# Holding weight loads back, one DMA server in the planner, and r and v loads issued from ScalarE

## The chip, the cores and the metric

The kernel runs on one core of one Trainium2 chip. The metric is device time in microseconds (us), the median of several executions. The span of a profile is about 2 us shorter than the time of its own execution (4 us below the median in the first profile of the kernel before, whose execution was a faster one); positions in a profile are counted from the start of the span.

Engine names: PE is TensorE's matmul, PEld its weight load, DVE is VectorE, ACT is ScalarE, POOL is GpSimd, SP is SyncE. A trailing q (SPq, ACTq) means the engine's sequencer, where DMA issues run.

## The reference

Two parts follow one another. A recurrence over 768 steps for 4 batches and 8 heads of 40 channels, and then a mixer over its output:

```python
for t in range(S):                                   # state: (B, H, D, D)
    y[:, :, t] = einsum('bhd,bhde->bhe', r_t, state)
    Sa = einsum('bhde,bhe->bhd', state, a_t)
    state = state * w_t[..., None] - einsum('bhd,bhe->bhde', Sa, b_t)
    state = state + einsum('bhd,bhe->bhde', v_t, k_t)
# x = y as (B, S, 320)
theta = x @ w_theta
u = x + w_tok_r @ (x * cos(theta)) + w_tok_i @ (x * sin(theta))   # over tokens
out = u + maximum(u @ w_ch, 0)
```

The kernel works on 24 chunks (4 batches of 6 chunks of 128 tokens). A chunk needs six loads of 160 KB (r, k, v, w, a, b): 144 loads. After the 6 chunks of a batch come the mixer rows of that batch.

## The kernel before

Every operation is entered in a planner, which simulates the engines and writes one static order for each engine. The kernel then issues the operations in that order. The parts that matter here:

```python
class Plan:
    def order(self, wait=47.7, tswitch=11847.0):
        ...
            elif o.work:                               # a DMA
                q = 0 if o.eng == "SP" else 1          # two servers: SP's and POOL's
                iss = 430 if o.eng == "SP" else 890
                free[o.eng] = t + iss
                s = max(dma[q], t + iss + 900)
                ...
                o.end = dma[q] + 1000
        ...
        out.sort(key=lambda o: (o.start, o.idx))
        return out
...
    raw_w = sb("raw_w", [128, H, D], FP32, 4)          # raw_a, raw_kb, raw_rv: four of each too
...
    def loads(i):                                      # w, k, b, a, r, v of chunk i
        for key, dst, src in load(i):
            add("SP", "load", i, lambda dst=dst, src=src: nc.sync.dma_start(out=dst, in_=src),
                430, [], [key], work=910)
...
    def prep(i):
        add("ACT", "ln", i, ...)        # lw <- raw_w, the first step of a chunk
        ...                             # cs (PE), exp (ACT), kb, ah (POOL, DVE for i < 2), rv casts
        tr("tkb", "ekb", ...); tr("ta", "ea", ...); tr("trv", "erv", ...)
                                        # transposes on PE, evictions kbT, aT, rvT on ACT
...
    def wtok_block(tb):                 # token weights: 2 rows of 192 KB in each of 6 blocks
        add("POOL", "wdma", i, ... nc.gpsimd.dma_start(...), 890, [], [...], work=1100)
...
    order = plan.order()
    for o in order:
        ...
        o.fn()
```

The `x0` matmuls (`ps_s<-rv,psi`) are the first step of a chunk's recurrence; I use their start as the clock of the pipeline. Chunk 8's `x0` comes at about the time when the first mixer rows (`ps_s<-zr,wtok_r`) start.

Of the kernel before, what the change touches and what calls it, by code (L numbers as in the profile page):

```python
# [12 lines left out]
ALU = mybir.AluOpType  # L13
# [4 lines left out]
LAT = {("PE", "ACT"): 36, ("PE", "DVE"): 38, ("ACT", "PE"): 52, ("DVE", "PE"): 52,  # L18
       ("POOL", "PE"): 53, ("ACT", "DVE"): 33, ("ACT", "POOL"): 77}
OVERLAP = {"ACT": 94, "DVE": 83, "POOL": 50}  # L20
FREE0 = {"PE": 800, "ACT": 2100, "DVE": 4400, "POOL": 3600, "SP": 740}
BANKS = 8
DOUBLE = 4


class Op:
    __slots__ = ("eng", "kind", "i", "fn", "cost", "tail", "reads", "writes", "prio",
                 "mode", "table", "new", "spare", "pre", "nsucc", "start", "end", "idx",
                 "npre", "succ", "work", "banks", "soft", "loose")


class Plan:
# [7 lines left out]
    def add(self, eng, kind, i, fn, cost, reads=(), writes=(), prio=0.0, mode=128,  # L40
            tail=0, table=None, new=None, spare=0, work=0, after=(), loose=False):
        o = Op()
        o.eng, o.kind, o.i, o.fn, o.cost, o.prio = eng, kind, i, fn, cost, prio
        o.mode, o.tail, o.table, o.new, o.spare, o.work = mode, tail, table, new, spare, work
        o.reads, o.writes, o.loose = reads, writes, loose
        o.idx = len(self.ops)
        pre = set(after)
        for r in reads:
            if r in self.writer:
                pre.add(self.writer[r])  # L50
        for w in writes:
            if w in self.writer:
                pre.add(self.writer[w])
            pre.update(self.readers.get(w, ()))
        for r in reads:
            self.readers.setdefault(r, []).append(o)
        for w in writes:
            self.writer[w] = o
            self.readers[w] = []
        pre.discard(o)  # L60
        o.pre = list(pre)
        self.ops.append(o)
        return o

    def order(self, wait=47.7, tswitch=11847.0):
        ops = self.ops
        for o in ops:
            o.succ = []
            o.npre = len(o.pre)
            o.start = o.end = None  # L70
            o.banks = None
        users = {}
        for o in ops:
            for k in set(o.reads) | set(o.writes):
                if k[0] == "ps":
                    users.setdefault(k, set()).add(o)
# [7 lines left out]
        for o in ops:  # L84
            for p in o.pre:
                p.succ.append(o)
            for p in o.soft:
                p.succ.append(o)
        left = {k: len(v) for k, v in users.items()}
# [8 lines left out]
        dma = [0.0, 0.0]  # L98
# [9 lines left out]
        def make_ready(o):  # L108
            t = 0.0
            for p in o.pre:  # L110
                t = max(t, lat(p, o))
            est0[o] = t
            ready[o.eng].append(o)
# [17 lines left out]
        while len(out) < n:  # L131
            pick = None
            for e, lst in ready.items():
                if not lst:
                    continue
                te = free[e]
                cand = []
                lo = None
                for o in lst:
                    t = max(te, est0[o])  # L140
                    b = None
                    if o.new is not None:
                        f = find(o)
                        if f is None:
                            continue
                        t = max(t, f[0])
                        b = f[1]
                    if e == "PE" and o.mode != mode:
                        t += 91
                    cand.append((t, o, b))  # L150
                    if lo is None or t < lo:
                        lo = t
# [3 lines left out]
                for t, o, b in cand:  # L156
                    s = o.prio + wait * (t - lo)
                    if e == "ACT" and o.table is not None and o.table != table:
                        s += tswitch
                    if best is None or (s, o.idx) < best[0]:  # L160
                        best = ((s, o.idx), t, o, b)
# [19 lines left out]
            elif o.work:  # L181
                q = 0 if o.eng == "SP" else 1
                iss = 430 if o.eng == "SP" else 890
                free[o.eng] = t + iss
                s = max(dma[q], t + iss + 900)
                if q == 1 and dma[0] > s:
                    dma[0] += o.work
                    dma[1] = s + 2 * o.work
                else:
                    dma[q] = s + o.work  # L190
                o.end = dma[q] + 1000
            else:
                o.end = t + o.cost
                free[o.eng] = o.end - OVERLAP[o.eng]
# [23 lines left out]
def tail(n):  # L218
# [3 lines left out]
OFF = dict(load=-32.72, ln=-14.21, cs=-14.27, exp=-12.91, kb=-24.2, ah=-17.45, rv=-8.81,  # L222
           tkb=-12.03, ekb=-12.49, ta=-6.68, ea=-13.73, spsi=-4.74, mpsi=3.81, sphi=-3.67,
           mphi=-0.3, trv=-7.1, erv=-4.13, slv=-1.2, mlv=12.94, x0=-1.29, nx=-1.28,
           nu=-1.19, enu=-4.96, gt=3.22, egt=5.53, gd=-0.91, egd=-4.34, nut=0.71,
           enut=-1.87, slu=0.59, mlu=4.85, y=4.31, ex=0.1, xt=7.27, ext=6.43, th=11.06,
           eth=17.93, sin=5.35, z=1.67, row=13.39, uadd=1.12, ut=13.16, eut=16.3, ch=19.9,
           oo=11.33, st=19.28, wdma=-32.85, wt=-13.25, ewt=-5.52)
PERIOD = 7.54
ROWLAG = 7.44  # L230
ROWSTEP = 7.6
# [3 lines left out]
def kernel(  # L235
# [130 lines left out]
    def prio(kind, i):  # L366
        return 1000.0 * (PERIOD * i + OFF[kind])

    def add(eng, kind, i, fn, cost, reads=(), writes=(), pr=None, **kw):
        return plan.add(eng, kind, i, fn, cost, tuple(reads), tuple(writes),  # L370
                        prio(kind, i) if pr is None else pr, **kw)
# [16 lines left out]
    def evac(eng, kind, i, psk, dst, n, reads=(), writes=()):  # L388
        if eng == "ACT":
            add(eng, kind, i, lambda: copy_words(dst, ps(psk)[:, 0:n // 2]),  # L390
                190 + n / 2.4, [psk], writes)
# [4 lines left out]
    def loads(i):  # L396
        for key, dst, src in load(i):
            add("SP", "load", i, lambda dst=dst, src=src: nc.sync.dma_start(out=dst, in_=src),  # L398
                430, [], [key], work=910)

    def prep(i):
# [6 lines left out]
            out=lw[:, :, 0:D], in_=raw_w[s4], func=AF.Ln), 465,  # L408
# [3 lines left out]
        def cs():  # L412
# [17 lines left out]
            out=ex, in_=ps(pk)[:, :, 0:328], func=AF.Exp), 740, [pk], [kex], table="lnexp")  # L430
# [3 lines left out]
        for j, nm in enumerate("kb"):  # L434
# [3 lines left out]
                490 if fast else 830, [("raw_" + nm, s4), kex], [("kb", j, i % NKB)])  # L438
# [3 lines left out]
            490 if fast else 830, [("raw_a", s4), kex], [("ah", i % 3)])  # L442
# [18 lines left out]
    def scores(i, kind, kindm, lhs, rhs, keys, dst, dkey, mask):  # L461
        p = ("ps", kind, i)

        def go():
# [7 lines left out]
        add("PE", kind, i, go, 8 * 28, keys, [p], new=(p, 2), mode=64, tail=tail(128))  # L472
# [3 lines left out]
            in1=mask.to_broadcast([128, 2 * G, 128]), op=ALU.mult), 1222, [p], [dkey])  # L476
# [11 lines left out]
    def recurrence(i):  # L488
# [9 lines left out]
        def x0():  # L498
# [16 lines left out]
            455, [pk], [("nx", s2)])  # L515

        def nu_mm():
# [8 lines left out]
            mul=-1.0), 480, [pk], [("nu", s2)])  # L526
        if not last:
            gk = ("ps", "gt", i)

            def gt_mm():  # L530
# [29 lines left out]
                340, [dk], [("gd", i % 2)])  # L560
# [5 lines left out]
    def x_transposed(kind, kinde, i, src, skey, dst, dkey, eng="ACT", pr=None):  # L566
        p = ("ps", kind, i)

        def go():
# [4 lines left out]
        add("PE", kind, i, go, 3 * mm(128), [skey], [p], pr=pr, new=(p, 1), tail=tail(128))  # L574
        d = dst.rearrange("p a b -> p (a b)")
        add(eng, kinde, i, lambda: copy_words(d, ps(p)[:, 0:192]), 345, [p], [dkey],
            pr=None if pr is None else pr + 500)

    def readout(i):
# [9 lines left out]
        def y():  # L589
# [21 lines left out]
            op=ALU.mult), 480, [pk, ("ex", i % NEX)], [("x", i % NX)])  # L611
# [7 lines left out]
    def theta(i):  # L619
# [4 lines left out]
        if i == N - 1:  # L624
            return
        add("ACT", "eth", i, lambda: nc.scalar.copy(out=th_t[0][:, j], in_=ps(pk)[:, 0:DM]),
            455, [pk], [("th", j)])

    def sines(bi, js):
        cs = cs_t[js[0] // 3]  # L630
        i = bi * NCH + js[-1]
        for c in range(2):
# [6 lines left out]
            else:  # L639
# [3 lines left out]
                    190 + 267 * len(js), [("th", j) for j in js],  # L643
# [16 lines left out]
    def mix_row(bi, j):  # L660
        q = bi * NCH + j
        base = 1000.0 * (PERIOD * (bi * NCH + NCH - 1) + ROWLAG + ROWSTEP * j + OFF["row"])
# [5 lines left out]
        for n, s in enumerate(order):  # L668
# [7 lines left out]
            if n == 0:  # L676
                need += [e for e in zk if e[3] <= (NT - 2 if bi < B - 1 else NT - 2)]
            add("PE", "row", q, chunk, 2 * mm(320), need, [pk], pr=base,
# [3 lines left out]
            out=u[:, 0:DM], in0=ps(pk)[:, 0:DM], in1=x[:, 0:DM], op=ALU.add), 480,  # L682
            [pk, ("x", q % NX)], [("u", q % 4)], pr=base + 1000 * (OFF["uadd"] - OFF["row"]))
        x_transposed("ut", "eut", q, u, ("u", q % 4), uT_t[q % 2], ("uT", q % 2),
                     pr=base + 1000 * (OFF["ut"] - OFF["row"]))
        ck = ("ps", "ch", q)
        add("PE", "ch", q, lambda: mix3(ps(ck)[:, 0:DM], uT_t[q % 2], wch), 3 * mm(320),
            [("uT", q % 2), ("wch", 0), ("wch", 1)], [ck], pr=base + 1000 * (OFF["ch"] - OFF["row"]),
# [4 lines left out]
            op1=ALU.add), 480, [ck, ("u", q % 4)], [("oo", q % 3)],  # L693
            pr=base + 1000 * (OFF["oo"] - OFF["row"]))
        add("SP", "st", q, lambda: nc.sync.dma_start(out=out_r[bi, j], in_=oo), 430,
            [("oo", q % 3)], [], pr=base + 1000 * (OFF["st"] - OFF["row"]), work=470)

    def mixer_weights():
        for dst, key, src in ((wth, "wth", moe_w_theta), (wch, "wch", moe_w_ch)):
# [5 lines left out]
            add("POOL", "wdma", 0, go, 890, [], [(key, 0)], work=500, pr=-500.0 if key == "wth" else 1e4)  # L705
            add("POOL", "wdma", 0, go2, 890, [], [(key, 1)], work=130, pr=-500.0 if key == "wth" else 1e4)

    def wtok_block(tb):
        i = 7 + tb
        for nm, ap in (("r", moe_w_tok_r), ("i", moe_w_tok_i)):  # L710
            row = wrow[nm][tb % 2]
            add("POOL", "wdma", i, lambda row=row, ap=ap: nc.gpsimd.dma_start(
                out=row, in_=ap[tb * 128:(tb + 1) * 128, :]), 890, [],
                [("wrow", nm, tb % 2)], work=1100)
# [86 lines left out]
```

## Time and profile before

| | before |
|---|---|
| time, median of 2 | 223.26 us |
| span | 219.2 us |
| first x0 | 16.7 us |
| x0 of chunk 8 | 76.4 us (7.5 us a chunk) |
| first mixer row | 73.6 us |

The page of the kernel before: busy time, then rows in which each digit is the busy share in tenths of one fortieth of the span.

```profile
PE 198.0 (90%) x3368; PEld 155.4 (71%) x3368; DVE 167.2 (76%) x250; ACT 147.1 (67%) x319; POOL 119.2 (54%) x184
...
PE   1519999889987999999999999999999999999992
...
PEclk9999999999999999999999999999999999999999
DMA  6999999999999899999999999999980000100121
```

The same in four stretches of time (start and end, length, then busy time of each engine with the number of instructions, clock, DMA share, GB/s), kernel before:

```profile
0.00:16.00 16.00, 4.49 (x44) 3.39 (x45) 7.72 (x47) 4.75 (x9) 6.78 (x20) 1.00 1.01 167
16.00:75.00 59.00, 53.28 (x993) 42.84 (x993) 47.58 (x57) 44.02 (x95) 36.82 (x56) 1.00 1.04 173
75.00:214.00 139.00, 138.90 (x2327) 108.74 (x2325) 110.48 (x144) 98.01 (x216) 75.59 (x109) 1.00 0.67 127
```

From 75 us on TensorE is the limit: 138.9 of 139 us. What can be won lies before, above all in the first 16 us. The chain of waits (start, length, what) says what holds the start up in the kernel before:

```profile
6.03 9.44 DMA raw_w<-in_w_dram
15.47 0.02 issue
15.50 0.48 ACT lw L407
```

w of chunk 1 takes 9.4 us to land, while GpSimd has asked for 968 KB of mixer weights besides w_theta. ScalarE meanwhile is early with chunk 0 (timeline: start, length, engine, line, operation; in brackets the idle time before it and what ended it), kernel before:

```profile
3.69 0.47 ACT L407 ACTIVATE lw<-raw_w 128x320 bf16<-128x320 f32 x1 [1.67 <-DMA raw_w<-in_w_dram]
...
9.17 0.37 ACT L383 COPY aT<-ps_s 128x256 f32<-128x256 f32 x1 [1.13 <-PE ps_s L380]
```

The PEclk row reads 9 from the start, and the stretches read 1.00, but the clock record of this run begins only at 21.9 us. Two groups of eight transposes, same shape, in the timeline of the kernel before:

```profile
6.38 1.04 PE L380 MATMUL ps_s<-ident,kb 128*128 128x128 bf16 x8 [1.34 <-DVE kb L436]
...
64.36 0.61 PE L380 MATMUL ps_s<-ident,rv 128*128 128x128 bf16 x8 [0.68 <-ACT nuT L383]
```

Their starts are 107 ns apart before 21.9 us and 56 ns after it: TensorE ran at half clock until then, and the PEclk row does not show it.

### The profile page before, as it was taken

The page shows a single profiled execution, that of the slowest core. Times are in us where ns is not written, and L with a number is a line of the kernel's source. Part 1 is how long each engine was busy: PE and PEld are TensorE (multiplying, and loading weights), DVE is VectorE, ACT ScalarE, POOL GpSimd, SP SyncE. Part 2 cuts the span into 40 slices and gives each one's busy share as a digit, 9 for nine tenths or more (in the row PEclk, how much of TensorE's full clock was granted, in tenths as well). Part 3 has the DMA queues.
Part 4 walks back from the last instruction along what each step waited for, and adds up shares of the span by engine and source line. Part 5 has one row for each costly group of instructions (what it writes and reads, how often), then busy time and mean ns, then how long its engine had stood idle before and what let it go on. Part 6 is the DMA issues. An engine that isn't in the chain of part 4 may idle for free.

```text
span 219.2 us, 8154 instructions
## 1 busy us (share of the span) xinstructions
PE 198.0 (90%) x3368; PEld 155.4 (71%) x3368; DVE 167.2 (76%) x250; ACT 147.1 (67%) x319; POOL 119.2 (54%) x184
## 2 busy tenths in 40 slices
PE   1519999889987999999999999999999999999992
PEld 1418778667776788878778778877877788776671
DVE  7336899885898759898598878869888889975532
ACT  3316755886769984996689766987698759563110
POOL 5600536798737791794938644986187507514000
PEclk9999999999999999999999999999999999999999
DMA  6999999999999899999999999999980000100121
GB/s 113 199 185 191 154 168 174 176 178 152 174 187 170 152 172 185 153 155 189 191 187 155 178 189 183 167 184 190 178 182 33 3 33 30 34 33 30 64 88 60
DMA packets 155684, 30.81 MB, mean 141 GB/s; under 512 B 150400, under 2 KB 155648, under 8 KB 155648
## 3 DMA queue, kind: packets, MB, share of 16 engines
q1 hardware_dynamic: 153216, 27.54, 68.9%
q0 software_dynamic: 2432, 2.77, 8.0%
q8 instruction: 26, 0.43, 0.8%
q14 instruction: 10, 0.08, 0.1%
HBM read 29.13 MB, written 3.93 MB: 151 GB/s over the span
## 4 chain that ended last, share of the span: by engine, by line
PE 74%; DMA 7%; DVE 6%; POOL 3%; ACT 3%; issue 3%; SPq 2%; DVEq 0%; ACTq 0%; POOLq 0%
PE ps_s L671 18%; PE ps_s L380 15%; PE ps_d L468 11%; PE ps_s L616 9%; DMA raw_w<-in_w_dram 7%; PE ps_s L572 4%; PE ps_s L538 2%; PE ps_s L520 2%; SPq L398 2%; PE ps_s L602 2%; PE ps_s L508 2%; DVE lamu L473 2%; PE ps_s L600 2%; DVE psi L473 2%; PE ps_s L502 1%
## 5 line engine op out<-in xcount | busy, mean ns | idle before, releaser
L436 POOL TENSOR_TENSOR kb<-raw_kb,ex 128x320 bf16<-128x320 f32 x44 | 37.1, 863 | 49.7 <-ACT ex L429 49.1
L671 PE MATMUL ps_s<-zr,wtok_r 128*128 128x320 bf16 x144 | 40.8, 300 | 0.0
L671 PE MATMUL ps_s<-zi,wtok_i 128*128 128x320 bf16 x144 | 40.7, 299 | 0.0
L473 DVE TENSOR_TENSOR lamu<-ps_d,mask_p 128x1024 bf16<-128x1024 f32 x24 | 29.3, 1221 | 5.3 <-PE ps_d L468 4.6
L473 DVE TENSOR_TENSOR psi<-ps_d,mask_p 128x1024 bf16<-128x1024 f32 x24 | 29.2, 1216 | 5.3 <-PE ps_d L468 5.3
L473 DVE TENSOR_TENSOR lamv<-ps_d,mask_p 128x1024 bf16<-128x1024 f32 x24 | 29.2, 1218 | 5.0 <-PE ps_d L468 2.7
L473 DVE TENSOR_TENSOR phi<-ps_d,mask_n 128x1024 bf16<-128x1024 f32 x24 | 29.3, 1219 | 1.9 <-PE ps_d L468 1.6
L445 POOL CAST rv<-raw_rv 128x320 bf16<-128x320 f32 x44 | 19.1, 452 | 16.0 <-DMA raw_rv<-in_r_dram 8.8
L652 POOL TENSOR_TENSOR zr<-cs,x 128x320 bf16<-128x320 f32 x23 | 17.9, 792 | 10.3 <-ACT cs L640 10.2
L383 ACT COPY rvT<-ps_s 128x512 f32<-128x512 f32 x24 | 14.2, 590 | 9.2 <-PE ps_s L380 9.0
L383 ACT COPY uT<-ps_s 128x192 f32<-128x192 f32 x24 | 7.7, 320 | 17.4 <-PE ps_s L572 13.9
L429 ACT ACTIVATE ex<-ps_d 128x656 f32<-128x656 f32 x24 | 17.2, 718 | 2.9 <-PE ps_d L424 2.0
L383 ACT COPY kbT<-ps_s 128x512 f32<-128x512 f32 x24 | 14.0, 584 | 7.5 <-PE ps_s L380 7.1
L440 POOL TENSOR_TENSOR ah<-raw_a,ex 128x320 bf16<-128x320 f32 x22 | 19.0, 866 | 0.0
L468 PE MATMUL ps_d<-aT,kbT 64*128 64x128 bf16 x384 | 18.3, 223 | 0.7 <-ACT aT L383 0.5
L380 PE MATMUL ps_s<-ident,kb 128*128 128x128 bf16 x192 | 15.9, 227 | 2.5 <-DVE kb L436 1.3
L652 POOL TENSOR_TENSOR zi<-cs,x 128x320 bf16<-128x320 f32 x23 | 17.9, 793 | 0.0
L681 DVE TENSOR_TENSOR u<-ps_s,x 128x320 bf16<-128x320 f32 x24 | 11.8, 490 | 8.0 <-PE ps_s L671 7.5
L671 PEld LDWEIGHTS <-wtok_r 128*128 128x128 bf16 x144 | 14.0, 98 | 4.5
L671 PEld LDWEIGHTS <-wtok_i 128*128 128x128 bf16 x144 | 14.1, 98 | 3.8
L407 ACT ACTIVATE lw<-raw_w 128x320 bf16<-128x320 f32 x24 | 11.2, 478 | 7.6 <-DMA raw_w<-in_w_dram 7.4
L691 DVE SCALAR_TENSOR_TENSOR oo<-ps_s,u 128x320 f32<-128x320 f32 x24 | 11.7, 488 | 5.8 <-PE ps_s L616 5.1
(109 smaller groups left out, 552.6 us busy)
## 6 DMA issues: line engine op xcount, KB each, us to landing
raw_w<-in_w_dram SPq DMA_DIRECT2D x24, 160.0 KB, 4.0
raw_kb<-in_k_dram SPq DMA_DIRECT2D x24, 160.0 KB, 4.1
raw_kb<-in_b_dram SPq DMA_DIRECT2D x24, 160.0 KB, 3.9
raw_a<-in_a_dram SPq DMA_DIRECT2D x24, 160.0 KB, 4.0
raw_rv<-in_r_dram SPq DMA_DIRECT2D x24, 160.0 KB, 3.9
raw_rv<-in_v_dram SPq DMA_DIRECT2D x24, 160.0 KB, 3.7
out_dram<-oo SPq DMA_DIRECT2D x24, 160.0 KB, 1.9
wrow_r<-in_moe_w_tok_r_dram POOLq DMA_DIRECT2D x6, 192.0 KB, 4.7
```

The lines of the kernel that those rows point to most:

```text
L380: nc.tensor.transpose(out=dst[:, c:c + 128], in_=pair(src, g), identity=ident)
L383: nc.scalar.copy(out=out.bitcast(FP32), in_=in_)
L429: add("ACT", "exp", i, lambda: nc.scalar.activation(out=ex, in_=ps(pk)[:, :, 0:328], func=AF.Exp), 740, [pk], [kex], table="lnexp")
L436: lambda j=j: (nc.vector if fast else nc.gpsimd).tensor_tensor(out=kb[:, j, :, 0:D], in0=raw_kb[s4][:, j], in1=invW, op=ALU.mult),
L440: lambda: (nc.vector if fast else nc.gpsimd).tensor_tensor(out=ah[:, :, 0:D], in0=raw_a[s4], in1=Wi, op=ALU.mult),
L445: lambda j=j: (nc.scalar.copy if fast else nc.gpsimd.tensor_copy)(out=rv[:, j, :, 0:D], in_=raw_rv[s4][:, j]),
L468: nc.tensor.matmul(t[:, q, g, :], lhsT=lhs[rows(q), g * 128:(g + 1) * 128], rhs=rhs[rows(q), g * 128:(g + 1) * 128], start=True, stop=True)
L473: add("DVE", kindm, i, lambda: nc.vector.tensor_tensor(out=dst.rearrange("p a b c -> p (a b) c"), in0=ps(p).rearrange("p a (g c) -> p (a g ...
L616: nc.tensor.matmul(dst, lhsT=lhs[:, kt, :], rhs=rhs[:, kt, :], start=kt == 0, stop=kt == 2)
L652: nc.vector if fast else nc.gpsimd).tensor_tensor(
L671: nc.tensor.matmul(ps(pk)[:, 0:DM], lhsT=wtok[nm][:, s, j * 128:(j + 1) * 128], rhs=zs[c][:, s], start=n == 0 and c == 0, stop=n == NT - 1 ...
L681: add("DVE", "uadd", q, lambda: nc.vector.tensor_tensor(out=u[:, 0:DM], in0=ps(pk)[:, 0:DM], in1=x[:, 0:DM], op=ALU.add), 480, [pk, ("x", ...
```

## The change

The intent: (1) hold the mixer weights back by release times, so that they don't stand in the way of the first chunks; (2) let the planner model all loads as served by one DMA server; (3) take the issue of r and v loads (46 of 144, all but chunk 0's) off SyncE and give it to ScalarE's DMA queue. All priorities were set anew with it.

```diff
+SP_DEPTH = 3600.0
...
-            t = 0.0
+            t = 0.0 if o.release is None else 1000.0 * TIMES["rel"][o.release]
...
                 te = free[e]
+                if e == "SP":
+                    te = max(te, dma - SP_DEPTH)
...
-                q = 0 if o.eng == "SP" else 1
-                iss = 430 if o.eng == "SP" else 890
-                free[o.eng] = t + iss
-                s = max(dma[q], t + iss + 900)
-                ...
+                free[o.eng] = t + o.cost
+                if o.eng in ("SP", "ACT"):
+                    dma = max(dma, t + 1350.0) + o.work
+                    o.end = dma + 600.0
+                else:
+                    s = max(t + 1800.0, dma - SP_DEPTH)
+                    dma = max(dma, s) + o.work
+                    o.end = min(dma, s + 2.0 * o.work) + 1000.0
...
     def loads(i):
         for key, dst, src in load(i):
-            add("SP", "load", i, lambda dst=dst, src=src: nc.sync.dma_start(out=dst, in_=src),
-                430, [], [key], work=910)
+            act = key[0] in ("raw_r", "raw_v") and i > 0
+            eng = nc.scalar if act else nc.sync
+            add("ACT" if act else "SP", "load", i,
+                lambda dst=dst, src=src, eng=eng: eng.dma_start(out=dst, in_=src),
+                100 if act else 650, [], [key], work=1030)
...
+            add("POOL", "wdma", 2 + tb, ..., 580, [], [...], at="rel", work=1240, release=2 + tb)
```

Note what the planner now believes: a load on SyncE waits until the server is less than 3.6 us behind; a load on ScalarE costs 0.1 us and never waits.

## The prediction

> **What bounds it now.** The page: span 219.2 us (time 223.26), TensorE busy 198.0 us (90%). Busy time by stretch: in 75–214 us TensorE is busy 138.9 of 139, clock 1.00, so that stretch is TensorE-bound. Before it, TensorE is busy 4.5 of the first 16 us and 53.3 of the next 59; the end leaves 4 us idle. So about 21 us are winnable, 11.5 of them in start-up. The chain of waits names the start-up: raw_w of chunk 1 is issued at 6.03 us and lands 9.4 us later, because GpSimd has queued the mixer weights and four 192 KB token-weight rows between 2.8 and 9 us. The queue of DMA issues shows SyncE's own issues at 2.8 and 3.8 us each there, 0.73 us median overall. Loads move at about 0.91 us per 160 KB (175–180 GB/s).
>
> **What changes.** Work on all compute engines is the same (3368 matmuls; switches between 64- and 128-row matmuls 136 to 132[...]). Moved:
> 1. Token weights and wch go out later. By itself: the 7.6 us of DMA they took early leave chunk 1's path; worth up to 5 us.
> 2. 46 of 144 loads (r, v from chunk 1 on) go to ScalarE's queue: at 0.5–0.7 us an issue, about 25–30 us more on ScalarE, busy 147 of 219 (80% in 75–175 us).
> 3. The whole static order changes.
>
> [...] DMA busy share of 0.97–1.19 before 150 us agrees: no bandwidth is gained. [...]
>
> **The step that decides.** ScalarE is in order, and the eight completion semaphores (the trace shows eight) are now shared by both issuers: each load waits for the one eight places earlier. In the new ScalarE order six r/v loads stand before the first ln, two of them waiting for earlier landings (ln of chunk 0 near 7.5 us instead of 3.7). Fifteen r/v loads, up to chunk 11, stand before the eviction of aT of chunk 0. The last of them needs r of chunk 7 landed and cast; that is the 29th load: about 2.75 + 29×0.91 + 1.3 (theta weights) = 30 us (estimate). In before aT of chunk 0 was evicted at 9.2 us and its x0 matmuls ran at 16.7; I expect these x0 matmuls at about 33 us. Loads of chunks 0–3 are then all there, so chunks go at 6.5–7.5 us each (7.5 in before). Mixer rows start after the x0 of chunk 8: at about 90–94 us against 73.6. From there before took 145.6 us; after has 94 matmuls fewer left: about 141.5. Sum 232–236 us span, plus 4 us outside the span.
>
> **Prediction: 237 us** (6% slower), range 227 to 250. Chances: faster by over 2% 0.09, within 2% 0.11, slower by over 2% 0.80.
>
> **Would show it right:** TensorE nearly idle until about 28–33 us; first x0 matmuls after 28 us; ScalarE idle or inside load issues then; loads of r for chunks 9–11 issued before aT of chunk 0; first mixer matmuls at 88–96 us; TensorE over 97% busy from 100 us on; ScalarE issues 0.5–1 us each. **Wrong:** first x0 matmuls before 22 us.
>
> **What would make it wrong.** ScalarE issues costing about 0.1 us and loads landing faster than 0.91 us; chunks 0–5 catching up at 5 us each since their data wait in SBUF (then 222–226); a faster dense stretch. On the other side: ScalarE, with its issues, becoming the limit in the dense stretch (245–250).

The sum runs: first x0 at about 33 us, first mixer row at about 90 to 94, 141.5 us from there to the end, so 232 to 236 us of span, and 4 us outside it (223.26 less 219.2). Two figures in it come from the trace of the kernel before: the first load landed at 3.66 us, that is 2.75 + 0.91. The 1.3 us for w_theta (200 KB; 1.1 us at 0.91 us per 160 KB) and the 0.5 to 0.7 us an issue were my estimates; SyncE's 144 load issues in that trace took 0.37 us at least and 0.73 us in the median.

## The result

| | before | after |
|---|---|---|
| time, median of 2 | 223.26 us | 258.23 us |
| span | 219.2 us | 257.4 us |
| first x0 | 16.7 us | 33.4 us |
| x0 of chunk 8 | 76.4 us | 110.9 us |
| from there to the end of the span | 142.8 us | 146.5 us |
| first mixer row | 73.6 us | 112.5 us |

The ratio is 1.160 (95% interval 1.150 to 1.171). Ratios here are the mean time of one kernel's fast runs over that of the other's of the same rounds, so not quite the ratio of the medians that I quote.

The 38.2 us of span (3 us more than the 35.0 us between the medians, see above) split into 16.7 us in the start, 17.8 us between x0 of chunk 0 and x0 of chunk 8 (77.5 against 59.7 us) and 3.7 us after it. The page of the kernel after:

```profile
PE 207.4 (81%) x3368; PEld 163.4 (63%) x3368; DVE 166.5 (65%) x250; ACT 147.2 (57%) x319; POOL 120.1 (47%) x184
...
PE   0341168969889639779999998999999989999993
...
PEclk9999999986999975999999999999999999999999
DMA  9999996798619999339479998999470000001112
```

The same work (3368 matmuls) takes 9.4 us more busy time, and the PEclk row has holes at the ninth and tenth and at the fifteenth and sixteenth digit. In stretches, kernel after:

```profile
0.00:33.00 33.00, 7.13 (x68) 5.25 (x68) 7.65 (x47) 6.42 (x12) 7.98 (x23) 1.00 1.36 175
33.00:112.50 79.50, 61.86 (x1044) 49.74 (x1045) 52.56 (x61) 46.14 (x99) 37.95 (x58) 0.89 0.84 134
112.50:252.00 139.50, 136.99 (x2254) 107.69 (x2250) 104.92 (x141) 94.00 (x207) 74.19 (x105) 1.00 0.53 100
```

The start is as predicted: DMA is never idle from 1.8 us on (175 GB/s, so two issuers move no more than one did at 167 to 173), but TensorE has nothing to do. ScalarE's timeline in the kernel after says why (ACTq rows are DMA issues):

```profile
25.69 0.58 ACT L399 COPY rvT<-ps_s 128x512 f32<-128x512 f32 x1 [3.01 <-DMA raw_w<-in_w_dram]
27.07 3.92 ACTq L417 DMA_DIRECT2D raw_rv<-in_r_dram  x3
31.02 0.37 ACT L399 COPY aT<-ps_s 128x256 f32<-128x256 f32 x1 [4.75 <-issue]
```

The eviction of aT of chunk 0, at 9.17 us before, comes at 31.02 us, behind fifteen r and v loads. ScalarE also waits for landings of loads that have nothing to do with its next operation (rvT "released" by raw_w). That is the wait of a load issue: in the trace the 168 loads and stores of both queues use eight completion semaphores in turn, 21 times each, and an issue waits for the load that had its semaphore before, eight places earlier in that turn. Of ScalarE's 14 issues that waited over 0.5 us, 12 went 0.02 to 0.10 us after that landing. The last of the fifteen, r of chunk 11, waited for its buffer: r of chunk 7 landed at 28.82 us, its cast on GpSimd ended at 29.41, and the issue began at 29.45.

The middle is not as predicted. ScalarE's two longest single waits from 33 to 112.5 us (engine, line, what it waited for, total, times, longest), kernel after; three groups of shorter waits, for TensorE's products, have more in total:

```profile
ACT nu L543 <- DMA raw_kb<-in_k_dram: 3.8, 1, 3.8
ACT rvT L399 <- DMA raw_w<-in_w_dram: 3.3, 1, 3.3
```

and the chain of waits of the kernel after in that place:

```profile
91.57 4.58 DMA raw_kb<-in_k_dram
96.14 0.03 ACTq L417
96.17 0.18 ACT nuT L399
96.36 0.05 issue
96.40 0.61 PE ps_d L487 x6
```

A k load lands, ScalarE's issue (ACTq) goes, the eviction behind it goes, TensorE goes. From x0 of chunk 0 (33.4 us) to 112.5 us ScalarE had 16 load issues; they were waited for 7.8 us, all of it between 84 and 102 us, and took 6.2 us (summed from the trace). And TensorE was at half clock until 45.7 us, at 56.0 to 62.8 and at 93.5 to 103.8 us: 29.4 us of the 77.5 between x0 of chunk 0 and of chunk 8. The transposes show it where the PEclk row does not (kernel after, compare with 0.61 us above):

```profile
39.64 1.26 PE L396 MATMUL ps_s<-ident,kb 128*128 128x128 bf16 x8
```

### The profile page after: what moved, and what is told of

It is laid out like the page before. It is cut to its first block, busy times and chain, and to the rows that moved or that the text cites. A ratio compares the mean times of both kernels' runs of the same rounds, so it can differ in the third digit from the quotient of the medians.

```text
span 257.4 us, 8139 instructions
## 1 busy us (share of the span) xinstructions
PE 207.4 (81%) x3368; PEld 163.4 (63%) x3368; DVE 166.5 (65%) x250; ACT 147.2 (57%) x319; POOL 120.1 (47%) x184
## 4 chain that ended last, share of the span: by engine, by line
PE 47%; ACT 6%; SPq 4%; DVE 3%; DMA 3%; issue 3%; POOL 2%; ACTq 0%; DVEq 0%; POOLq 0%
PE ps_s L688 14%; PE ps_s L396 8%; PE ps_s L634 6%; PE ps_d L487 5%; SPq L417 4%; PE ps_s L591 3%; DMA raw_kb<-in_k_dram 2%; ACT L658 2%; PE ps_s L539 2%; ACT cs L658 1%; DVE psi L492 1%; PE ps_s L620 1%; PE ps_s L557 1%; DMA raw_w<-in_w_dram 1%; PE ps_s L618 1%
## 5 line engine op out<-in xcount | busy, mean ns | idle before, releaser
L464 POOL CAST rv<-raw_rv 128x320 bf16<-128x320 f32 x44 | 19.8, 460 | 47.1 <-PE ps_s L557 17.3
L459 POOL TENSOR_TENSOR ah<-raw_a,ex 128x320 bf16<-128x320 f32 x22 | 19.0, 863 | 20.9 <-issue 17.1
L487 PE MATMUL ps_d<-aT,kbT 64*128 64x128 bf16 x384 | 17.8, 225 | 12.5 <-ACT aT L399 12.2
L670 POOL TENSOR_TENSOR zr<-cs,x 128x320 bf16<-128x320 f32 x23 | 17.8, 795 | 20.2 <-ACT cs L658 20.1
L399 ACT COPY rvT<-ps_s 128x512 f32<-128x512 f32 x24 | 14.1, 589 | 22.7 <-PE ps_s L396 8.4
L487 PEld LDWEIGHTS <-kbT 64*128 64x128 bf16 x384 | 12.1, 98 | 17.1 <-issue 14.9
L698 DVE TENSOR_TENSOR u<-ps_s,x 128x320 bf16<-128x320 f32 x24 | 11.7, 489 | 14.2 <-PE ps_s L688 12.9
L670 POOL TENSOR_TENSOR zi<-cs,x 128x320 bf16<-128x320 f32 x23 | 17.8, 796 | 0.1
L399 ACT COPY uT<-ps_s 128x192 f32<-128x192 f32 x24 | 7.6, 318 | 17.8 <-PE ps_s L591 17.6
L396 PE MATMUL ps_s<-ident,kb 128*128 128x128 bf16 x192 | 16.6, 233 | 1.4 <-DVE kb L455 1.3
L396 PE MATMUL ps_s<-ident,rv 128*128 128x128 bf16 x192 | 17.2, 242 | 0.6 <-ACT rv L464 0.6
L618 PE MATMUL ps_s<-kb,lamv 128*128 128x40 bf16 x192 | 16.2, 185 | 1.0 <-DVE lamv L492 1.0
L533 ACT CAST nx<-ps_s 128x320 bf16<-128x320 f32 x24 | 10.2, 425 | 11.9 <-PE ps_s L527 9.8
L399 ACT COPY kbT<-ps_s 128x512 f32<-128x512 f32 x24 | 14.1, 587 | 5.0 <-PE ps_s L396 4.8
```

The source lines that it names most:

```text
L396: nc.tensor.transpose(out=dst[:, c:c + 128], in_=pair(src, g), identity=ident)
L399: nc.scalar.copy(out=out.bitcast(FP32), in_=in_)
L459: lambda: (nc.vector if fast else nc.gpsimd).tensor_tensor(out=ah[:, :, 0:D], in0=raw_a[s4], in1=Wi, op=ALU.mult),
L464: lambda j=j: (nc.scalar.copy if fast else nc.gpsimd.tensor_copy)(out=rv[:, j, :, 0:D], in_=raw_rv[s4][:, j]),
L487: nc.tensor.matmul(t[:, q, g, :], lhsT=lhs[rows(q), g * 128:(g + 1) * 128], rhs=rhs[rows(q), g * 128:(g + 1) * 128], start=True, stop=True)
L618: nc.tensor.matmul(o, lhsT=lamv[:, p, g, :], rhs=kb[:, 0, h, 0:D], start=first, stop=False, skip_group_check=True)
```

## The experiments

Sixteen kernels ran, all correct. The times of the kernel before beside them were 222.17, 223.03, 223.06 and 222.71 us, so these medians differ by 0.4% (the first two are of the same chip). This table is the key to all of it. "Half clock" is the time between x0 of chunk 0 and x0 of chunk 8 in which TensorE's clock was at half, and in brackets how long TensorE was busy in it. The last three columns come from one profiled execution of each kernel. In e4 the first mixer row comes 15.1 us before x0 of chunk 8, so its 92.7 us hold mixer work too.

| run | time us | ratio | first x0 | x0 chunk 0 to 8 | half clock (busy) |
|---|---|---|---|---|---|
| before | 223.26 | | 16.7 | 59.7 | 5.2 (4.9) |
| after | 258.23 | 1.160 | 33.4 | 77.5 | 29.4 (24.0) |
| e1_all_sp | 220.08 | 0.991 | 11.5 | 57.9 | 5.8 (5.7) |
| e2_same_order_sp | 238.81 | 1.076 | 24.5 | 64.8 | 5.5 (5.4) |
| e3_before_rv_scalar | 239.74 | 1.080 | 20.8 | 72.5 | 21.8 (13.8) |
| e4_scalar_gated | 259.57 | 1.168 | 19.3 | 92.7 | 27.0 (24.7) |
| e5_deep_raw | 260.29 | 1.168 | 35.3 | 75.8 | 20.2 (14.0) |
| e6_paced_scalar | 256.66 | 1.153 | 20.8 | 67.1 | 8.7 (8.7) |
| e7_late_scalar | 235.28 | 1.054 | 11.8 | 61.1 | 6.5 (6.3) |
| e8_weights_not_held | 239.99 | 1.074 | 15.8 | 72.1 | 26.2 (22.6) |
| f1_first_15_scalar | 241.97 | 1.084 | 26.9 | 65.3 | 8.5 (8.3) |
| f2_other_31_scalar | 249.47 | 1.118 | 23.5 | 77.1 | 21.2 (17.6) |
| f3_dummy_scalar | 225.70 | 1.012 | 10.9 | 59.1 | 7.1 (6.7) |
| f4_before_weights_held | 223.53 | 1.000 | 12.5 | 64.2 | 12.1 (11.4) |
| g1_after_filled | 257.27 | 1.158 | 37.5 | 71.6 | 4.1 (4.1) |
| g2_late_scalar_filled | 230.28 (two fast runs) | 1.034 | 11.2 | 62.7 | 10.2 (9.4) |
| g3_sp_filled | 219.32 | 0.984 | 10.4 | 57.3 | 0.0 (0.0) |
| g4_before_filled | 223.25 | 1.003 | 17.1 | 60.5 | 6.8 (6.8) |

### e1: the change without ScalarE's loads

```diff
-            act = key[0] in ("raw_r", "raw_v") and i > 0
+            act = False
```

> The changed kernel with its new planner, new numbers and held-back weights, but all 144 loads planned for and issued by SyncE. Theory A (ScalarE's queue: its r/v loads are priced at 0.1 us and have no depth limit in the planner, so they stand ahead of ScalarE's own compute and block it): the 35 us and more go away, time at most 223 us, first x0 matmuls of chunk 0 before 18 us, mixer rows start before 76 us. Theory B (the re-fitted numbers or the single-server planner give a bad order, whoever issues): 240 us or more. Theory C (only the issue time on ScalarE, 46 times 0.4 to 0.7 us): 230 to 240 us.

Measured: 220.08 us (219.31 to 220.48), ratio 0.991 (0.985 to 0.997). The rest of the change (planner, priorities, held weights) is worth 0.9%, within the 2% that count as the same. It starts 5.2 us earlier than before, but its first mixer row comes at 76.7 us, 3.1 us later than before. The ScalarE loads carry the loss, either as issues or through the plan that they lead to.

### e2: the changed kernel's order, SyncE as the issuer

```diff
-            eng = nc.scalar if act else nc.sync
+            eng = nc.sync
```

> The changed kernel's plan unchanged (the planner still thinks that ScalarE issues r and v), but the 46 loads are really issued by SyncE, in the plan's order. ScalarE can no longer block on a load. If the blocking of ScalarE is what costs: first x0 near 24 us (load of a of chunk 0 stands 17th in SyncE's queue now), time 235 to 248 us. If the planned order itself (loads for later chunks ahead of what is needed now) costs it all: within 2% of 258 us. If nothing but ScalarE's blocking cost: below 228 us.

Measured: 238.81 us, ratio 1.076 (1.068 to 1.083). So of the 38 us between e1 and the kernel after, about 19 come from the order (a planner that takes ScalarE loads as nearly free puts too many in front), and about 19 from the issuer. In the middle, 64.8 of the 77.5 us remain: the order costs 5.1 us there against before, the issuer 12.7 us.

### e3: the order of before, ScalarE as the issuer

```diff
-            add("SP", "load", i, lambda dst=dst, src=src: nc.sync.dma_start(out=dst, in_=src),
+            act = key[0] in ("raw_r", "raw_v") and i > 0
+            eng = nc.scalar if act else nc.sync
+            add("SP", "load", i, lambda dst=dst, src=src, eng=eng: eng.dma_start(out=dst, in_=src),
                 430, [], [key], work=910)
```

> The kernel before with its planner, numbers and static order; only the 46 r and v loads from chunk 1 on are issued by ScalarE instead of SyncE, each at the place where the plan has it. Theory A in its wide form (any load in ScalarE's in-order queue blocks its compute through shared semaphores[...]): slower by 3 to 10%, 230 to 245 us, most of it before 75 us. Theory A in its narrow form (only the order of the new plan is at fault) : 221 to 227 us. Theory C: 226 to 232 us.

Measured: 239.74 us, ratio 1.080 (1.072 to 1.087). The issuer alone costs 8% in an order that is good with SyncE. ScalarE waited 20.3 us before its 46 issues, 17.3 of them before 35 us.

### e4: a gate for ScalarE's loads in the planner

```diff
+                    if e == "ACT" and o.work:
+                        t = max(t, dma - SP_DEPTH)
                     cand.append((t, o, b))
```

> The changed kernel with one line more in the planner: a load on ScalarE is not planned before the DMA server is within the same 3.6 us that already hold SyncE back. ScalarE still issues the 46 loads. Theory A: the runs of loads ahead of compute are gone from ScalarE's queue (2 before the first ln, 6 before aT of chunk 0), first x0 near 18 us, time 218 to 230 us. Theory B: 240 us or more. Wide form of A: between, 230 to 240 us.

Measured: 259.57 us. The start is mended (19.3 us), and nothing is won: the middle takes 92.7 us. The theory that the loss is just the run of loads in front of chunk 0 falls. In this new plan ScalarE still waited 13.5 us before its 46 issues; that these waits make its long middle isn't shown.

### e5: deeper buffers for SyncE's loads

```diff
-    raw_w = sb("raw_w", [128, H, D], FP32, 4)            # raw_a, raw_kb alike
+    raw_w = sb("raw_w", [128, H, D], FP32, 7)            # index i % 7, order as planned for 4
```

> The changed kernel with the same order on every engine, but seven buffers instead of four for the tensors that SyncE loads (w, k, b, a); r and v keep four. It is to say what makes chunks 0 to 8 go at 9.7 us each in the changed kernel. Theory (a ring of waits): SyncE's loads wait for buffers whose release stands behind ScalarE's held-up stream, and ScalarE's own load issues wait for SyncE's landings. Then SyncE's waits before its loads between 33 and 112 us fall from 53 us to below 20, the x0 matmuls of chunk 8 come at most 67 us after those of chunk 0 (77.5 in the changed kernel), the mixer rows start before 102 us (112.5) and the time is at most 248 us. The start stays (x0 of chunk 0 at 32 to 35 us). Rival (ScalarE's own issues and their waits hold up the compute, the buffers don't matter): 74 to 80 us from x0 of chunk 0 to that of chunk 8, time 254 to 262 us.

Measured: 260.29 us, the middle 75.8 us. SyncE's waits before its loads from 33 to 112 us fell by half (24.8 us in sum, 53.2 in the kernel after, 4.4 in before from 16 to 75 us), and the middle hardly moved. The waits fell less than the theory asked for (below 20 us), but halving them moved the middle by only 1.7 us, so the ring of waits through the buffers is at most a small part; the rival's numbers hold.

### e6: each ScalarE load behind the aT eviction four chunks earlier

```diff
-                100 if act else 650, [], [key], work=1030)
+                100 if act else 650, [], [key], work=1030,
+                after=((evicted[i - 4],) if act and i >= 4 else ()))
```

> The changed kernel, but the r and v loads of chunk i stay on ScalarE only behind the eviction of aT of chunk i-4, so none of them can stand in front of compute that the start needs. Theory (place in ScalarE's stream is what costs, not the issuer): first x0 at 17 to 20 us, ScalarE waits before its issues below 6 us in sum (20.8 in the changed kernel), chunks 0 to 8 at 7.3 to 8 us each, mixer rows from 76 to 83 us, time 222 to 230 us. Rival (a load issued by ScalarE costs its issue and its wait wherever it stands, as the kernel with the gate suggests): chunks at 9 us or more, rows after 90 us, time above 238 us.

Measured: 256.66 us. Theory and its numbers missed: the start was mended (20.8 us) and the middle took 67.1 us, yet from its first row (94.4 us) to the end it took 159.2 us against 144.9 in the kernel after. ScalarE still waited 17.6 us before its issues, 9.2 of them after 112.5 us. This plan differs in every engine, and I didn't follow its late part further.

### e7: e1's order, only the 30 late r and v loads on ScalarE

```diff
-            eng = nc.scalar if act else nc.sync                    # e1, where act is False
+            eng = nc.scalar if key[0] in ("raw_r", "raw_v") and i > 8 else nc.sync
```

> The plan of the all-SyncE version (220.08 us), order unchanged on every engine, but the 30 loads of r and v of chunks 9 to 23 are issued by ScalarE. Theory (an issue costs only where compute behind it in ScalarE is on the chain; in the dense stretch TensorE is the limit): the x0 matmuls of chunks 0 to 7 within 1 us of the all-SyncE version, the time 219 to 224 us. Rival (each issue costs its 0.4 to 0.7 us and its wait on a loaded ScalarE everywhere): 30 issues add 12 us or more, the time is above 229 us.

Measured: 235.28 us, ratio 1.054: 15 us more than e1, and my theory fell. The order is identical to e1's, so one can lay the two traces side by side, instruction by instruction. They agree within 0.4 us until 69 us. ScalarE's timeline of e7_late_scalar:

```profile
67.70 0.49 ACT L426 ACTIVATE lw<-raw_w 128x320 bf16<-128x320 f32 x1
71.47 0.42 ACTq L417 DMA_DIRECT2D raw_rv<-in_r_dram  x1
71.99 0.37 ACT L399 COPY nuT<-ps_s 128x256 f32<-128x256 f32 x1 [3.79 <-DMA raw_w<-in_w_dram]
```

and the same place of e1_all_sp:

```profile
67.43 0.49 ACT L426 ACTIVATE lw<-raw_w 128x320 bf16<-128x320 f32 x1
67.84 0.37 ACT L399 COPY nuT<-ps_s 128x256 f32<-128x256 f32 x1
```

One issue waited 3.3 us for a w load to land, and nuT, which has nothing to do with it, went 4.15 us later. TensorE's longest wait from 66 to 100 us in e7_late_scalar is for that nuT:

```profile
PE ps_s L396 <- ACT nuT L399: 2.9, 1, 2.9
```

When TensorE goes on, at 72.4 us, its clock is at half for 10.2 us (the PEclk row of e7_late_scalar):

```profile
PEclk9999999999997589999999999999999999999999
```

Laid beside e1, TensorE is 3.3 us behind at 72.4 us and 6.6 us behind at 82.7, where the half clock ends; then it stays at 6.6 us until 90 us, and later waits at full clock bring it to 8.7 us at 97 and 14.3 at the end. So a wait of 3.3 us had become 6.6 by the end of the half clock, and nearly 8 us of the loss came after it. The wait is not in the bar that the profile draws for the issue: the bar is 0.42 us, and the 3.28 us of waiting stand in front of it as idle time.

### e8: e1 with the weights not held back

```diff
-            t = 0.0 if o.release is None else 1000.0 * TIMES["rel"][o.release]
+            t = 0.0
```

> The all-SyncE version (220.08 us, first x0 at 11.5 us, rows at 76.7 us) with the release times of the mixer weights ignored, so GpSimd asks for them when it is free. What holding the weights back is worth: if the start's gain is kept, first x0 goes to 16 to 18 us and the time up by 3 to 5 us, to 223 to 225. If the gain is given back later (the all-SyncE version starts 5 us before the kernel before and its rows still start 3 us after it), first x0 at 15 to 18 us and the time within 1.5 us of 220.

Measured: 239.99 us, outside both. First x0 came at 15.8 us as said, but x0 of chunk 1 only at 34.4 us, and TensorE was at half clock from 28.4 to 42.0 us. The planner made another plan with it (mixer rows first at 110.8 us), so this is no clean measure of the hold-back; it says that the new priorities and the release times belong together. f4 is the clean one.

### f1 and f2: the changed kernel's order, 15 or 31 of the loads on ScalarE

```diff
+            first = i < 10 if key[0] == "raw_r" else i < 7
-            eng = nc.scalar if act else nc.sync
+            eng = nc.scalar if act and first else nc.sync          # f1; f2: "and not first"
```

> The changed kernel's order on every engine; of its 46 r and v loads only the 15 that stand in front of the first aT eviction are issued by ScalarE, the other 31 by SyncE. This is what the prediction had costed. If the prediction's picture holds for these 15 (only its pace was wrong, and the wrong pace comes from the other 31): first x0 at 32 to 35 us, the mixer rows at 97 to 102 us, time 245 to 250 us. If the loss of the middle comes from the late start itself (loads and compute out of step, the clock at half), the rows come at 108 us or later and the time is above 254 us.

> The other half: the changed kernel's order, the 15 first r and v loads issued by SyncE and the 31 others by ScalarE. If each issue that ScalarE has to wait for is passed on to TensorE wherever it stands: first x0 at 24 to 26 us as with SyncE alone, but rows at 100 to 105 us (91.0 with SyncE alone) and time 247 to 254 us. If these 31 cost nothing by themselves: rows at 90 to 94 us and time 238 to 242 us.

The edit is not quite what I had written. By the planner's order (built again from the kernel after) the fifteen loads in front of the aT eviction are r and v of chunks 1, 2, 3, 5, 6 and 7 and r of 9, 10 and 11; the edit takes r of 1 to 9 and v of 1 to 6, so only twelve of them. It leaves out v of 7 and r of 10 and 11, and takes r and v of 4 and r of 8 in their place. The traces agree: ScalarE issues twelve loads before aT of chunk 0 in f1 and three in f2 (at 12.31, 15.07 and 17.80 us).

Measured: f1 241.97 us, f2 249.47 us; e2, with the same order and all on SyncE, 238.81 us. f2 settles where the middle's loss comes from: with twelve of the first fifteen on SyncE the first x0 is at 23.5 us, no later than in e2 (24.5), and the middle still takes 77.1 us, as in the kernel after (77.5), against 64.8 in e2. So loads that the prediction had counted as free in the middle (28 of its 31 are on ScalarE here) cost it 12.3 us. ScalarE's first two groups of waits from 33 to 112.5 us in f2_other_31_scalar are both landings that its next operation does not need:

```profile
ACT rvT L399 <- DMA raw_w<-in_w_dram: 4.6, 1, 4.6
ACT th L645 <- DMA raw_a<-in_a_dram: 4.2, 1, 4.2
```

In e2 no landing is among the first groups; the largest there is

```profile
ACT rvT L399 <- PE ps_s L396: 5.1, 7, 1.3
```

f1 missed its first number: first x0 at 26.9 us, not 32 to 35, with 0.2 us of waits in ScalarE. In f1 SyncE had to issue the other r and v loads at their planned (too early) places and stood still from 2.6 to 11.9 and from 12.9 to 19.0 us, so fewer loads were under way. The issues at 11.9 us (v of chunk 7) and from 19.0 us on (r of 10 and of 11, with r of 0 between them) include the three that the edit had left on SyncE: here SyncE did the waiting that held ScalarE in the kernel after. So f1 is no test of what the prediction had costed. The halves don't add up (3.2 + 10.7 us against 19.4); with both on ScalarE the first x0 is 6.5 us later than in f1.

### f3: ScalarE's time without its waits

```diff
+    def issue(dst, src, more):
+        nc.sync.dma_start(out=dst, in_=src)
+        if more:                                         # r, v of chunks 9 to 23
+            nc.scalar.copy(out=idle[1], in_=idle[0])     # 128x320, no dependence
```

> The all-SyncE version (220.08 us), with a copy of 128x320 numbers on ScalarE (about 0.43 us, no wait) at each of the 30 places where the version with late ScalarE loads (235.28 us) has a load issue on ScalarE. The loads stay on SyncE. It separates ScalarE's occupied time from its waits. If the waits for an earlier landing (and what the clock does after them) make the 15 us: at most 223 us. If the occupied time makes them, since ScalarE feeds a TensorE that is the limit: 229 us or more.

Measured: 225.70 us, between the two expectations: 5.6 us for thirty copies (0.46 us each by the trace), against 15.2 us for thirty load issues in the same places, whose bars sum to 14.0 us. (By the ratios to the kernels before of the same rounds: 4.6 against 14.1 us.) So about 10 of the 15 us are not the occupied time but the waits and what follows from them. The 5.6 us say that ScalarE is not free in the dense stretch either; in the profiled run, laid beside e1, 2.4 us of them came while the clock was at half from 72.6 to 79.4 us.

### f4: the kernel before with the weights held back

```diff
     order = plan.order()
+    # POOL: probe <- raw_a[1] (8 elements), then the first two token rows;
+    # wch and the next two rows behind kb of chunk 2
```

> The kernel before, order unchanged but for GpSimd's weight loads: the first two token-weight rows wait for the landing of a of chunk 1 (through an 8-element copy), wch and the next two rows stand behind GpSimd's kb products of chunk 2. What holding weights back is worth by itself. If the start's gain is kept: raw_w of chunk 1 lands by 12 us (15.5 in the kernel before), first x0 at 12 to 14 us (16.7), time 3 to 5 us under that of the kernel before of the same rounds. If it is given back: first x0 as said, the mixer rows not before 72 us (73.6) and the time within 1.5 us.

Measured: 223.53 us, ratio 1.000 (0.995 to 1.004). First x0 at 12.5 us (16.7) and x0 of chunk 1 at 20.0 (24.2), but x0 of chunk 2 at 30.9 (31.0): the 4.2 us are given back within one chunk. TensorE waited 2.2 us for ah of chunk 2 and then ran at half clock from 24.6 to 31.5 us. Holding the weights back is worth nothing by itself in this order.

### g1 and g2: TensorE kept busy through the waits

```diff
+    def filler(o):      # overwritten by the instruction that follows
+        for _ in range(FILL[o.kind, o.i]):
+            nc.tensor.matmul(dst, lhsT=ntri_inc, rhs=ntri_inc, start=True, stop=True)
...
+        if o.eng == "PE" and (o.kind, o.i) in FILL:
+            filler(o)
         o.fn()
```

> The changed kernel, loads and orders unchanged, with 389 filler matmuls of 128 columns in TensorE's stream in front of instructions that were seen to wait (190 and 10 of them before the first psi products, 45 and 34 before the two long waits at 89 and 94 us); each writes the bank that the next instruction overwrites. Theory (about half of the middle's loss is TensorE at half clock: it was busy 24.0 us at half clock between x0 of chunk 0 and of chunk 8, 5.4 us in the same order with SyncE alone, so up to 9.3 us): the half-clock time of that stretch falls from 29 us to below 12, x0 of chunk 0 stays at 32 to 35 us, x0 of chunk 8 comes 67 to 72 us later (77.5), time 248 to 253 us. Rival (the clock is only a symptom, ScalarE's waits set the pace): 75 to 80 us from chunk 0 to 8, time 256 to 262 us.

> The version whose 30 late r and v loads are issued by ScalarE (235.28 us), with 40, 20 and 28 filler matmuls in front of the three instructions that waited 2.9, 1.6 and 2.1 us at 70, 76 and 136 us. Theory (clock): no half clock from 72 to 83 us, 3 to 4 us less, 231 to 233 us. Rival (waits and occupied time alone): 234.5 us or more.

Measured, g1: half clock in the middle down from 29.4 to 4.1 us, and the middle from 77.5 to 71.6 us. So about 5.9 of the 12.7 us that the issuer costs in the middle were the clock. One could object that the later start alone had shortened the middle. But laid beside the kernel after, instruction by instruction, g1 gains 1.3, 1.5 and 3.1 us in stretches where it is at full clock and the other at half (39.5 to 45.7, 56.0 to 62.8 and 93.5 to 103.8 us), 5.9 in sum. The rest cancels: 1.3 us gained before 36 us, where a load issue of 1.94 us holds ScalarE in the kernel after, and 1.4 us lost at 90 us. The time was 257.27 us, though, not 248 to 253: the start slipped by 4.1 us (first x0 at 37.5 us), because r of chunk 5 was issued by ScalarE at 17.82 us instead of 12.93. With the fillers in the program that load had got another semaphore: the one that b of chunk 1 had before it, which landed at 17.74 us (17.96 in the kernel after), and not that of r of chunk 3, which had landed at 12.54. So which landing an issue waits for can change with an edit that touches no load. The PEclk row of g1_after_filled, with the half clock now only up to 41.7 us:

```profile
PEclk9855977999999999999999999999999999999999
```

Measured, g2: 229.16 and 231.4 us in the two fast runs, 235.73 and 238.61 in two that count as slow; ratio of the fast ones 1.034 (1.026 to 1.042) against 1.054 (1.048 to 1.061) of e7. By these fast runs it is 4 to 5 us faster, with 88 matmuls of extra work; but its four runs spread over 9 us, and with all of them the median is 233.57 us, so this gain is likely, not shown. In the profiled run, the fastest, the half clock at 72 us is gone (g2_late_scalar_filled):

```profile
PEclk9995899999999999999999999999999999999998
```

The wait of ScalarE stays; what TensorE loses to e1 between 69 and 97 us of e1's time falls from 8.7 us in e7 to 3.2. (Half clock from 18.0 to 24.8 us, which e7 does not have, cost this run 2.0 us before.)

### g3 and g4: the same in kernels that don't stall later

The edit is that of g1, with 71 fillers in e1's kernel and 98 in the kernel before, all in the first 20 us.

> The all-SyncE version (220.08 us), with 71 filler matmuls in TensorE's waits of the first 20 us. Its transposes stand 106 ns apart until 17.2 us. Theory (the start too is slowed by the clock): full clock before 10 us, x0 of chunk 1 by 20 us (21.0), time 1.5 to 4 us less, 216 to 218.5 us. Rival (the start is bound by landings and by the way from engine to engine): time within 1 us of 220.

> The kernel before, with 98 filler matmuls in TensorE's waits of the first 16 us (50 of them in front of the first products of chunk 1, which waited 4.4 us). Its transposes stand 107 ns apart until 21.9 us. Theory (clock): full clock by 12 us, 1.5 to 4 us less than the kernel before of the same rounds. Rival (landings of chunks 1 and 2 set the start): within 1 us.

Measured, g3: 219.32 us (217.60 to 220.02, 6 runs), ratio to before 0.984 (0.980 to 0.989). This is the best version that ran; it beats both kernels, before by 1.6% (less than 2%, so the verdict reads unclear, but the interval lies below 1). Its clock record begins at 5.0 us at full clock, and x0 of chunk 1 is at 19.4 us (21.0 in e1). The gain over e1 is about 0.7% by the two ratios, from different chips, and their intervals overlap, so that gain is likely, not shown. The profiled run is the fastest of the six and the only one with a mean clock of 1.000 (0.992 in the others). In it g3 gains 1.6 us on e1 within the first 18 us, while e1 is at half clock.

Measured, g4: 223.25 us, ratio 1.003: nothing. The full clock came at 5.7 us, but in the profiled run it fell to half again from 19.3 to 22.7 and from 50.0 to 53.5 us. In the kernel before the start is set by the landings of chunk 1 and not by the clock; the rival's number holds.

## Why the prediction was wrong, point by point

- **What bounds before: right.** TensorE from 75 us on; what can be won lies in the start.
- **No bandwidth is gained by a second issuer: right.** 175 GB/s over the first 33 us after, 167 to 173 before. An issue took 0.375 us on ScalarE's queue (median) and 0.72 us on SyncE's before, and no time was won by moving it. (The DMA shares that the prediction gives as 0.97 to 1.19 read 0.90 to 1.23 in its 5 us stretches from 5 to 75 us.)
- **The start: right, in mechanism and size.** Fifteen loads in front of the aT eviction, the last of them behind the landing of r of chunk 7 (28.82 us; the 28th load to land, 29th predicted); aT predicted at 30 us, measured 31.02; x0 of chunk 0 predicted at about 33 us, measured 33.4; the first ln predicted near 7.5 us, measured 8.87.
- **The dense end: nearly right.** 141.5 us from the first mixer row to the end predicted, 144.9 measured; TensorE busy 98% of 112.5 to 252 us.
- **The pace of the middle: wrong. This is the step that failed:** "Loads of chunks 0–3 are then all there, so chunks go at 6.5–7.5 us each (7.5 in before)." They went at 9.7 us. The premise held (the last load of chunks 0 to 3 landed at 30.3 us), but even x0 of chunk 3 came 31.5 us after that of chunk 0. The first mixer row came at 112.5 us instead of 90 to 94, and those 18 to 22 us are nearly the whole miss of the total, 21 us.

I had counted ScalarE's waits only for the loads in front of chunk 0, and the issues of the other 31 loads as time that ScalarE could spare. What the runs showed in its place, between x0 of chunk 0 and x0 of chunk 8:

1. The order itself costs 5.1 us over before (e2: 64.8 against 59.7 us). What in the order does it was not followed.
2. ScalarE as the issuer costs 12.3 to 12.7 us (f2: 77.1, after: 77.5, e2: 64.8). An issue that has to wait for the load eight places earlier holds the evictions behind it, and TensorE's next instruction waits for one of those. e7 shows one such case from end to end: 3.28 us of waiting before the issue, nuT 4.15 us later, 2.9 us of waiting in TensorE. Not every issue does it: in the kernel after, all 7.8 us of waits lie between 84 and 102 us, and two of them, before 91.36 and 94.92 us, put TensorE 5.8 us further behind e2.
3. About 5.9 us of that are TensorE's clock (g1: 71.6 us). The half clock up to 45.7 us follows the empty start, and that from 56.0 to 62.8 us no wait of ScalarE's issues; only that from 93.5 us stands at the long waits. The remaining 6 to 7 us are the waits and the occupied time; f3 shows in another order that waits and their consequences outweigh occupied time.

The prediction names the clock only for 75 to 214 us of the kernel before ("clock 1.00"), where the record covers it. That the clock could fall to half, as it is in the first 21.9 us of the kernel before, has no part in its pace.

The half clock at 56.0 us in the kernel after sets in without a single wait of over 1 us just before it. The traces say what to look at instead: TensorE was busy for only 53% of the 3.4 us before 56.0 us. (3.4 us is how long a half clock of g4 lasted, from 19.3 to 22.7 us; others lasted 6.8 us, here from 56.0, 10.2 in e7 and 13.6 in e8.) By my count over all the profiles (without the last 5 us of each) the clock fell 32 times; TensorE had been busy 5 to 69% of the 3.4 us before, and in 15 cases no gap in them was over 1 us. In the kernel after, a stretch as empty as the one before 56.0 us also passed without a fall (52% busy in the 3.4 us up to 111.8 us), so this share alone does not say when the clock falls. What is measured is that it fell after many short gaps (none over 0.95 us before 56.0 us) as well as after a long one (2.9 us in e7).

What stays open: what in the new order costs 5.1 us in the middle; and why e6's late part is slow.

## What to carry to other kernels

Here the issues were cheap on SyncE, whose stream holds only loads and stores: with all 144 loads there the new plan took 220.08 us (e1), with 30 of them on ScalarE in the same order 235.28 (e7). On ScalarE, which works in order, the price of an issue was not only its bar in the profile but also the wait in front of it (f3 against e7: 5.6 and 15.2 us). In the kernel after ScalarE waited 20.8 us in sum before its 46 issues, and 12 of the 14 waits of over 0.5 us ended with the landing of another load, the one that had the same completion semaphore before. And before a gap in TensorE's stream is priced at its own length, look at the distance of equal transposes after it: in e7 a gap of 2.9 us was followed by 10.2 us at half clock.
